# Attention and gate block in one kernel: values ahead of the second softmax with a fixed order of VectorE and GpSimd, front steps in pairs, and products of half of block 2 summed on GpSimd

## Chip, cores, metric

One core of one Trainium2 chip. The metric is the device time of one execution in microseconds (us). Every run that is compared was fast (only one core runs, and no run was over 1.5% above the fastest of its kernel). Engines: PE is TensorE, DVE is VectorE, ACT is ScalarE, POOL is GpSimd, SP issues most transfers.

## The reference, cut

```python
def _A_ref(x, wqkv, wo):                 # S=2048, D=640, 32 heads of 20
    W, dil = 8, 2                        # each position looks at 8 positions, 2 apart, itself and back
    q, k, v = ...(x @ wqkv)
    logits = einsum("bhsd,bhswd->bhsw", q, kg) * Dh**-0.5     # masked where the index is below 0
    attn = softmax(logits, axis=-1)                           # over the 8 offsets
    o = einsum("bhsw,bhswd->bhsd", attn, vg)
    return o.reshape(B, S, D) @ wo
def _B_ref(x, w_gate, w_up, w_down):     # F=1536
    return ((x @ w_gate) * (x @ w_up)) @ w_down
xn = layernorm(x)
return x + _A_ref(xn, wqkv, wo) + _B_ref(xn, w_gate, w_up, w_down)
```

## The kernel before

The sequence is cut into four blocks of 512 positions, 0 to 3. A small scheduler in the kernel's own Python code lists every instruction, orders the engines by modelled durations and sets the semaphores; dependencies come from overlapping memory.

**Logits.** DVE multiplies queries by shifted keys (a product of four offsets at once, 2048 elements). PE sums a product over the 20 columns of each head with a matrix of ones, G, in four 32-column matmuls. There are five chunks of 128 columns; for a half of the offsets in `QUAD`, four of the five are first added in fp32, by GpSimd and by transfers that add to their destination, so that PE has one sum instead of four. Before, that was block 3 alone.

```python
QUAD = {3: (1, 0)}                              # block: halves of the offsets summed on GpSimd
ORDER = ((0, "n"), (1, "n"), (2, "n"), (3, "n"), (3, "w"))
...
for a in range(4):                              # logits(): four 32-column matmuls for each product
    e.matmul(o, G[:], x, start=(i == 0), stop=(i == nt - 1), tile_position=(0, 32 * a))
```

**Softmax.** Blocks 0 and 1 share one logit tile, blocks 2 and 3 the second, LOG1. After a softmax, 16 transfers on SP's queue move the weights into ATX, with the offsets spread over the partitions as the value sums need them.

```python
def move():
    for a in range(4):
        for q in range(4):
            src = L[32 * a:32 * a + 32]...      # L = LOG[x]
            d = ATX[x][32 * q:32 * q + 32]...
            dma(d, src, r=[src], w=[d], ...)
    mark("atx", x)
```

**Shared memory.** Buffers that aren't needed at the same time lie over one another. The gate products of block 2 lie over the two logit tiles. HX0 to HX3 lie over LOG0, HX4 to HX7 over LOG1. The last four gate chunks of block 2 use HX4 to HX7. ACT evacuates gate results into them, and may not do so before the moves out of LOG1 have landed.

```python
LOG = [sb(f"LOG{i}", [128, 2, W, TS]) for i in range(2)]
HX = [sb(f"HX{i}", [128, JB], at=place[0] - 8192 + i * 1024) for i in range(8)]
...
HXM = (0, 1, 2, 3, 8, 9, 10, 11, 4, 5, 6, 7)    # gate chunk of block 2 -> buffer
...
if j == 2 and m == 8:
    yield have("atx", 1)                        # the moves are issued; their landing is a semaphore wait
```

Of the kernel before, what the change touches and what calls it, by code (L numbers as in the profile page):

```python
# [49 lines left out]
class Sched:  # L50
# [5 lines left out]
    def __init__(self, nc):  # L56
# [7 lines left out]
        self.t_lock = 0.0  # L64
        self.t_data = 0.0
# [42 lines left out]
    def deps_of(self, eng, rk, wk):  # L108
# [6 lines left out]
        for k in wk:  # L115
            st = self.state.get(k)
            if st is None:
                continue
            o, rds = st
            if o is not None and not (eng == "pe" and o.eng == "pe"):  # L120
                deps[o.idx] = o
            for q in rds:
                if inorder and q.eng == eng and not q.dma and eng != "dve":
                    continue
                deps[q.idx] = q
        return deps

    def op(self, eng, fn, r=(), w=(), dma=False, name="", occ=None, lat=None, lock=False, nbytes=0, mode=0, group=None, extra=0.0, acc=0.0, land=None):
# [7 lines left out]
        deps = self.deps_of(eng, rk, wk)  # L136
        if occ is None and not dma:
            occ = 0.1
# [45 lines left out]
        if dma:  # L184
# [7 lines left out]
            else:  # L192
                g = self.groups[group]
                g[1].append(X)
                X.event = (g[0], 16)
        self.ops.append(X)
# [152 lines left out]
def build_kernel(nc, A_x, A_wqkv, A_wo, B_x, B_w_gate, B_w_up, B_w_down, out):  # L349
# [43 lines left out]
    sv_free = list(range(NS))  # L393
# [21 lines left out]
    QUAD = {3: (1, 0)}  # L415
# [47 lines left out]
    def dma(o, i, r=(), w=(), name="", eng="sp", group=None, land=None):  # L463
# [10 lines left out]
       r=[IDENT[:]], w=[IDENT[:]], name="ident", occ=0.4)  # L474
    op("pool", lambda e: e.memset(G[:], 0.0), w=[G[:]], name="g0", occ=0.2)
# [58 lines left out]
    def front(t):  # L534
# [11 lines left out]

        def sqrt():
            op("act", lambda e: e.activation(sd, mv[:, 1:2], ACT.Sqrt, bias=EPSC[:, 0:1]), r=[("mv", t), EPSC[:]],  # L548
               w=[("sd", t)], name=f"sd{t}", occ=0.25)
            mark("sd", t)  # L550

        def recip():
            op("dve", lambda e: e.reciprocal(rstd, sd), r=[("sd", t)], w=[("rstd", t)], name=f"rstd{t}", occ=0.16)
            mark("rstd", t)
            if t >= N_DVE_A:
                op("dve", lambda e: e.tensor_scalar(nmr, mv[:, 0:1], rstd, -1.0, op0=ALU.mult, op1=ALU.mult),
                   r=[("mv", t), ("rstd", t)], w=[("nmr", t)], name=f"nmr{t}", occ=0.13)
# [27 lines left out]
        yield Task("act", sqrt, r=[("mv", t)], prio=p - 1)  # L585
        yield Task("dve", recip, r=[("sd", t)], prio=p)
# [192 lines left out]
    def calm():  # L779
        return all(("sm", x) in done or count.get(("logits", x), 0) < 2 for x in range(2))  # L780

    def tokens():
        return [("tok", x) for x in range(2) if ("sm", x) in done]
# [7 lines left out]
    def products():  # L791
        rows = {j: [] for j in range(NJ)}
        holds = {}
        for j, kind in ORDER:
# [4 lines left out]
            else:  # L799
                if len(QUAD.get(j, ())) == 2 and j not in holds:  # L800
# [4 lines left out]
            if len(rows[j]) == 10 - 3 * len(QUAD.get(j, ())):  # L805
                K.spawn(logits(j, rows[j]))

# [17 lines left out]
    def q_bank(j, c, hold):  # L825
# [7 lines left out]
        def copy():  # L833
            evac([(QT[:, j, c, :], PS[:, hold[0], :], JB)], f"qev{j}_{c}")
# [13 lines left out]
    def wide(j, slots, hold):  # L848
        halves = [(r, q0) for r in QUAD[j] for q0 in (0, 2)]
        acc, parts = {}, {1: [], 0: []}  # L850
        for c0 in (0, 2):
            for i, (r, q0) in enumerate(halves):
                f = []
                for c in (c0, c0 + 1):
                    yield lambda: len(hold[c]) > 0 and len(usable(j)) > 0
                    k = slot(j)
# [6 lines left out]
                    def go(o=o, qb=qb, kv=kv, q=q, rk=rk):  # L863
                        X = op("dve", lambda e: e.tensor_tensor(o[:], qb, kv, ALU.mult), r=[q, rk], w=[o[:]],  # L864
# [50 lines left out]
    def logits(j, slots):  # L915
# [7 lines left out]
        def go(*bs):  # L923
            for i, e in enumerate(slots):
                n, s, r = e[:3]
                b, i, nt = bs[1 - r], i - (0 if r else n1), n1 if r else len(slots) - n1
                for a in range(4):
                    o = PS[32 * a:32 * a + 32, b, :].rearrange("p (q s) -> p q s", q=4)
                    x = s[:, :, a * TS:(a + 1) * TS]
                    op("pe", (lambda o, x, i, a: lambda e: e.matmul(o, G[:], x, start=(i == 0), stop=(i == nt - 1),  # L930
                                                                   tile_position=(0, 32 * a)))(o, x, i, a),
# [25 lines left out]
    def softmax(x):  # L957
        def tt(o, a, b, f, name, occ):
            return Task("dve", lambda: op("dve", lambda e: e.tensor_tensor(o, a, b, f), r=[a, b], w=[o], name=name, occ=occ,
                                          lock=True), r=[a, b], w=[o], prio=10, lock=True)  # L960
# [8 lines left out]
        def sub():  # L969
            op("dve", lambda e: e.tensor_tensor(L[:], L[:], bc(M3[:], 8), ALU.subtract), r=[L[:], m3], w=[L[:]], name="lsub",  # L970
               occ=1.2, lock=True)

        def exp():
            op("act", lambda e: e.activation(L[:], L[:], ACT.Exp), r=[L[:]], w=[L[:]], name="exp", occ=1.9)

        def recip():
            op("act", lambda e: e.activation(s3, s3, ACT.Ln), r=[s3], w=[s3], name="rln", occ=0.4)
            op("act", lambda e: e.activation(R, s3, ACT.Exp, scale=-1.0), r=[s3], w=[R], name="rs", occ=0.4)
# [431 lines left out]
```

## Time and profile before

| | before |
|---|---|
| time, median of 4 runs | 268.65 us (268.47 to 268.70) |
| span of the profiled run | 266.8 us |
| start of PE's first transpose, start of its last group | 5.28, 263.72 us |
| second softmax's last multiply starts | 129.75 us |

The prediction below shows the page, PE's waits and the groups. Read the table with them: PE's first transpose to its last group is 258.4 us of the span, and it is nearly gapless in there.

The timeline of ACT shows where the first gate results go into the memory that they read:

```profile
152.11 0.60 ACT L660 ACTIVATE HX<-PS 128x512 bf16<-128x512 f32 x1 [1.56 <-PE PS L1195]
```

This is the ninth of block 2's twelve gate chunks, the first that goes to HX4. In brackets is the idle time before it and what ended it: ACT waited for PE alone. The last move landed at 142.7, 1.9 us after the start of its issue, and had been over for 9.4 us.

### The profile page before, as it was taken

The page shows a single profiled execution, that of the slowest core. Times are in us where ns is not written, and L with a number is a line of the kernel's source. Part 1 is how long each engine was busy: PE and PEld are TensorE (multiplying, and loading weights), DVE is VectorE, ACT ScalarE, POOL GpSimd, SP SyncE. Part 2 cuts the span into 40 slices and gives each one's busy share as a digit, 9 for nine tenths or more (in the row PEclk, how much of TensorE's full clock was granted, in tenths as well). Part 3 has the DMA queues.
Part 4 walks back from the last instruction along what each step waited for, and adds up shares of the span by engine and source line. Part 5 has one row for each costly group of instructions (what it writes and reads, how often), then busy time and mean ns, then how long its engine had stood idle before and what let it go on. Part 6 is the DMA issues. An engine that isn't in the chain of part 4 may idle for free.

```text
span 266.8 us, 4468 instructions
## 1 busy us (share of the span) xinstructions
PE 261.3 (98%) x1771; PEld 152.6 (57%) x1788; DVE 218.3 (82%) x278; ACT 107.6 (40%) x193; POOL 132.4 (50%) x83
## 2 busy tenths in 40 slices
PE   7999999999999999999999999999999999999996
PEld 5996965444444444444444446764577547754775
DVE  4678899999999996379999899988998999981221
ACT  3469998556732122255434442007500460016000
POOL 1000000000007359700399999977999799979000
PEclk9999999999999999999999999999999999999999
DMA  7974789502226997193426733656345633130101
GB/s 213 374 207 81 195 107 371 213 0 98 101 49 161 192 234 178 9 333 81 114 49 142 170 80 87 185 162 168 80 129 152 184 96 89 49 98 2 49 27 49
DMA packets 40933, 35.75 MB, mean 134 GB/s; under 512 B 16080, under 2 KB 39120, under 8 KB 40912
## 3 DMA queue, kind: packets, MB, share of 16 engines
q1 hardware_dynamic: 40096, 33.31, 46.0%
q0 software_dynamic: 576, 2.10, 4.1%
q8 instruction: 14, 0.23, 0.4%
q10 hardware_dynamic: 240, 0.05, 0.1%
q14 instruction: 7, 0.06, 0.1%
HBM read 25.07 MB, written 5.26 MB: 114 GB/s over the span
## 4 chain that ended last, share of the span: by engine, by line
PE 96%; DVE 1%; DMA 1%; issue 1%; ACT 0%
PE PS L1195 39%; PE PS L1277 28%; PE PS L655 22%; PE PS L930 3%; PE PS L687 2%; PE PS L1144 2%; DMA XST<-in_A_x_dram 1%; PE PS L599 0%; DVE STATS L542 0%; ACT XNT L611 0%; DVE XNS L563 0%; DVE XNT L609 0%; DVE FOUT L1290 0%; ACT SD L548 0%; DVE MV L545 0%
## 5 line engine op out<-in xcount | busy, mean ns | idle before, releaser
L1096 POOL TENSOR_TENSOR SV<-PV 128x1024 bf16<-128x1024 f32 x40 | 93.2, 2361 | 20.4 <-DVE LOG L981 19.4
L1091 DVE TENSOR_TENSOR PV<-VX,PS 128x1024 f32<-128x1024 bf16 (+1 forms) x56 | 91.9, 1669 | 2.5 <-POOL SV L1096 2.3
L655 PE MATMUL PS<-XNT,WQKV 128*128 128x512 bf16 (+2 forms) x384 | 60.2, 315 | 0.4 <-issue 0.2
L1195 PE MATMUL PS<-XNT,WG 128*128 128x512 bf16 x238 | 59.4, 379 | 0.2
L1195 PE MATMUL PS<-XNT,WU 128*128 128x512 bf16 x231 | 57.7, 379 | 0.4 <-issue 0.2
L655 PEld LDWEIGHTS PS<-XNT,WQKV 128*128 128x128 bf16 x390 | 37.9, 112 | 21.8 <-ACT LOG L941 0.8
L1195 PEld LDWEIGHTS PS<-XNT,WG 128*128 128x128 bf16 x240 | 23.3, 98 | 28.5 <-issue 0.8
L1195 PEld LDWEIGHTS PS<-XNT,WU 128*128 128x128 bf16 x240 | 23.4, 98 | 28.2 <-ACT LOG L941 0.4
L819 DVE TENSOR_TENSOR PRD<-QT,KT 128x2048 bf16<-128x2048 bf16 x32 | 36.8, 1215 | 0.0
L1290 DVE TENSOR_TENSOR FOUT<-PS,XR 128x320 bf16<-128x320 f32 (+1 forms) x33 | 15.7, 477 | 18.4 <-PE PS L1277 18.3
L1277 PE MATMUL PS<-WD,HT 128*128 128x320 bf16 x192 | 28.5, 299 | 0.0
L660 ACT ACTIVATE HT<-PS 128x512 bf16<-128x512 f32 x24 | 14.3, 596 | 31.6 <-PE PS L1195 31.6
L1277 PE MATMUL PS<-WO,OT 128*128 128x320 bf16 (+1 forms) x165 | 26.6, 295 | 0.0
L890 POOL TENSOR_TENSOR PRF<-PRF,PRF 128x1024 f32<-128x1024 f32 x4 | 9.4, 2348 | 31.2 <-DVE PRF L864 31.2
L660 ACT ACTIVATE UX<-PS 128x512 bf16<-128x512 f32 x14 | 8.4, 597 | 39.5 <-PE PS L1195 39.5
L949 POOL MEMSET LOG<- 32x6 bf16 (+6 forms) x7 | 0.4, 96 | 47.6 <-ACT LOG L941 47.6
L1204 DVE TENSOR_TENSOR HT<-HT,PS 128x512 bf16<-128x512 bf16 x23 | 15.7, 684 | 9.5 <-PE PS L1195 7.4
L1277 PEld LDWEIGHTS PS<-WD,HT 128*128 128x128 bf16 x192 | 18.6, 98 | 8.0 <-issue 0.4
L1277 PEld LDWEIGHTS PS<-WO,OT 128*128 128x128 bf16 x165 | 15.9, 98 | 5.9
L864 DVE TENSOR_TENSOR PRF<-PS,KT 128x1024 f32<-128x1024 f32 x16 | 19.0, 1216 | 0.3 <-DMA PRF<-PRF 0.3
L660 ACT ACTIVATE XNT<-PS 128x512 bf16<-128x512 f32 x12 | 7.2, 598 | 25.5 <-PE PS L1195 25.5
L542 DVE BATCH_NORM_STATS2 STATS<-XST 128x6 f32<-128x320 bf16 x32 | 14.6, 472 | 2.5 <-DMA XST<-in_A_x_dram 2.5
(62 smaller groups left out, 235.7 us busy)
## 6 DMA issues: line engine op xcount, KB each, us to landing
VX<-v_scratch SPq DMA_DIRECT2D x80, 130.0 KB, 2.9
XST<-in_A_x_dram SPq DMA_DIRECT2D x16, 160.0 KB, 5.7
v_scratch<-VST SPq DMA_DIRECT2D x4, 640.0 KB, 4.2
XR<-in_A_x_dram SPq DMA_DIRECT2D x16, 160.0 KB, 2.7
out_dram<-FOUT SPq DMA_DIRECT2D x15, 160.0 KB, 1.8
PRF<-PRF POOLq DMA_DIRECT2D x4, 512.0 KB, 8.7
WG<-in_B_w_gate_dram SPq DMA_DIRECT2D x1, 1920.0 KB, 8.6
WU<-in_B_w_up_dram SPq DMA_DIRECT2D x1, 1920.0 KB, 12.0
```

The costliest lines, as they stand in the source:

```text
L542: op("dve", lambda e: e.bn_stats(o, a), r=[a], w=[("st", t, i)], name=f"bn{t}_{i}", occ=0.49)
L655: op("pe", (lambda o, l, x, c, first: lambda e: e.matmul(o, l, x, start=first, stop=(c == NCH - 1)))(o, l, x, c, first), r=[l, x], w=[o], ...
L660: X = op("act", (lambda o, i: lambda e: e.activation(o, i, ACT.Copy))(o, i), r=[i], w=[o], name=name, occ=0.12 + n * 0.9e-3)
L819: op("dve", lambda e: e.tensor_tensor(s[:], qb, kv, ALU.mult), r=[q, rk], w=[s[:]], name=f"prod{j}_{r}_{c}", occ=1.15, lock=True)
L864: X = op("dve", lambda e: e.tensor_tensor(o[:], qb, kv, ALU.mult), r=[q, rk], w=[o[:]], name=f"prow{j}_{r}_{c}_{q0}", occ=1.17)
L890: yield Task("pool", lambda: op("pool", lambda e: e.tensor_tensor(x, x, y, ALU.add), r=[x, y] + tokens(), w=[x], name=name, occ=2.36, lock ...
L1091: op("dve", lambda e: e.tensor_tensor(p, vw, a, ALU.mult), r=[vv] + rk, w=[p], name=f"pv{u}_{x}_{r0}", occ=0.09 + 1.1 * nr)
L1096: X = op("pool", lambda e: e.tensor_tensor(o, p[:, :, 0, :], p[:, :, 1, :], ALU.add), r=[p[:]] + tokens(), w=[o], name=f"pva{u}_{x}", occ= ...
L1195: op("pe", (lambda l, x, c: lambda e: e.matmul(PS[:, b, :], l, x, start=(c == 0), stop=(c == NCH - 1)))(l, x, c), r=[l, x], w=[PS[:, b, :] ...
L1204: X = op("dve", lambda e: e.tensor_tensor(h, h, PS[:, hold[1], :], ALU.mult), r=[h, PS[:, hold[1], :]], w=[h], name=f"h{m}_{j}", occ=0.65)
L1277: op("pe", (lambda l, x, i: lambda e: e.matmul(dst, l, x, start=(i == 0), stop=(i == n - 1)))(l, x, i), r=[l, x], w=[PS[:, b, :]], name=f" ...
L1290: X = op("dve", lambda e: e.tensor_tensor(o, PS[:, b, 0:wid], xr, ALU.add), r=[PS[:, b, :], xr], w=[o], name=f"fin{t}_{nb}", occ=0.15 + wi ...
```

## The change

The intent: take logit matmuls off PE by adding half of block 2's products on GpSimd, and make room for that. GpSimd stood 19.4 us before the second softmax ended; now its first value sums come before that softmax and between its steps. The order of the DVE and GpSimd instructions that the program marks with `lock` is fixed by semaphores instead of by timing (the port order below, after the program's name `port`). The layer norm's small steps are done for two row tiles at once.

```diff
-    QUAD = {3: (1, 0)}
+    QUAD = {2: (1,), 3: (1, 0)}
-    ORDER = ((0, "n"), (1, "n"), (2, "n"), (3, "n"), (3, "w"))
+    ORDER = ((0, "n"), (1, "n"), (2, "w"), (2, "n"), (3, "n"), (3, "w"))
 ...  (fixed port order: each side waits for what the other issued before)
+        if lock:
+            deps.update({d.idx: d for d in self.port["pool" if eng == "dve" else "dve"]})
 ...  (values may start before the last logits; GpSimd work only where it fits ahead of the next softmax step)
-    def calm():
-        return all(("sm", x) in done or count.get(("logits", x), 0) < 2 for x in range(2))
+    def room(occ, ready=0.0):
+        def f():
+            if count.get(("logits", 0), 0) >= 2 and ("sm", 0) not in done:
+                return False
+            return due[0] == INF or max(K.t["pool"], K.t_lock, ready) + occ <= due[0] + SLIP
+        return f
 ...
     def vx_loads():
-        yield num(NJ, "lg")
+        yield have("products")
 ...  (front in pairs)
+    GROUPS = ((4, 5), (6, 7), (8, 9), (10, 11), (12, 13), (14, 15))
 ...  (the selector SEL is built on GpSimd instead of DVE; further parts cut)
```

More of the change, by code (lines that the diff above doesn't have):

```diff
@@ L64, in __init__ @@
         self.t_lock = 0.0
+        self.port = {"dve": [], "pool": []}
         self.t_data = 0.0
@@ L122, in deps_of @@
             for q in rds:
-                if inorder and q.eng == eng and not q.dma and eng != "dve":
+                if inorder and q.eng == eng and not q.dma and eng != "dve" and not (eng == "act" and k[0] == "ps"):
                     continue
@@ L195, in op @@
                 X.event = (g[0], 16)
+        if lock:
+            self.port[eng] = [X] if eng == "dve" else self.port[eng] + [X]
+            if eng == "dve":
+                self.port["pool"] = []
         self.ops.append(X)
@@ L392, in build_kernel @@
     SV += [sb(f"SV{5 + i}", [128, 4, JB], at=a_ra + i * 4096) for i in range(3)]
-    sv_free = list(range(NS))
+    sv_free = [3, 4, 0, 1, 2]
     a_sc = place[0]
@@ L474, in build_kernel @@
        r=[IDENT[:]], w=[IDENT[:]], name="ident", occ=0.4)
+    op("pool", lambda e: e.memset(SEL[:], 0.0), w=[SEL[:]], name="sel", occ=0.1)
+    for q in range(4):
+        op("pool", (lambda q: lambda e: e.affine_select(SEL[:], SEL[:], pattern=[[-1, 32]], compare_op=ALU.not_equal, fill=1.0,
+                                                        base=-32 * q, channel_multiplier=1))(q),
+           r=[SEL[:]], w=[SEL[:]], name=f"sel{q}", occ=0.2)
     op("pool", lambda e: e.memset(G[:], 0.0), w=[G[:]], name="g0", occ=0.2)
@@ L545, in aggr @@
             op("dve", lambda e: e.bn_aggr(mv, st), r=[("st", t, 0), ("st", t, 1)], w=[("mv", t)], name=f"bnag{t}", occ=0.2)
+        ts = next((g for g in GROUPS if t in g), (t,))
+        t0, t1 = ts[0], ts[-1] + 1
         def sqrt():
-            op("act", lambda e: e.activation(sd, mv[:, 1:2], ACT.Sqrt, bias=EPSC[:, 0:1]), r=[("mv", t), EPSC[:]],
-               w=[("sd", t)], name=f"sd{t}", occ=0.25)
-            mark("sd", t)
+            o, i = SD[:, t0:t1, 0:1], MV[:, t0:t1, 1:2]
+            op("act", lambda e: e.activation(o, i, ACT.Sqrt, bias=EPSC[:, 0:1]), r=[("mv", k) for k in ts] + [EPSC[:]],
+               w=[("sd", k) for k in ts], name=f"sd{t}", occ=0.25)
+            for k in ts:
+                mark("sd", k)
         def recip():
-            op("dve", lambda e: e.reciprocal(rstd, sd), r=[("sd", t)], w=[("rstd", t)], name=f"rstd{t}", occ=0.16)
-            mark("rstd", t)
+            o, i = SD[:, t0:t1, 1:2], SD[:, t0:t1, 0:1]
+            op("dve", lambda e: e.reciprocal(o, i), r=[("sd", k) for k in ts], w=[("rstd", k) for k in ts], name=f"rstd{t}", occ=0.16)
             if t >= N_DVE_A:
-                op("dve", lambda e: e.tensor_scalar(nmr, mv[:, 0:1], rstd, -1.0, op0=ALU.mult, op1=ALU.mult),
-                   r=[("mv", t), ("rstd", t)], w=[("nmr", t)], name=f"nmr{t}", occ=0.13)
+                n, m = SD[:, t0:t1, 2:3], MV[:, t0:t1, 0:1]
+                op("dve", lambda e: e.scalar_tensor_tensor(n, m, -1.0, o, op0=ALU.mult, op1=ALU.mult),
+                   r=[x for k in ts for x in (("mv", k), ("rstd", k))], w=[("nmr", k) for k in ts], name=f"nmr{t}", occ=0.13)
+            for k in ts:
+                mark("rstd", k)
         def apply():
@@ L584, in front @@
         yield Task("dve", aggr, r=[("st", t, 1)], prio=p)
-        yield Task("act", sqrt, r=[("mv", t)], prio=p - 1)
-        yield Task("dve", recip, r=[("sd", t)], prio=p)
+        mark("mv", t)
+        if t == ts[-1]:
+            yield Task("act", sqrt, r=[("mv", t)], prio=p - 1)
+            yield Task("dve", recip, r=[("sd", t)], prio=p)
+        yield have("rstd", t)
         if t >= NXN:
@@ L777, in slot @@
         return n
-    def calm():
-        return all(("sm", x) in done or count.get(("logits", x), 0) < 2 for x in range(2))
+    INF = 1e9
+    due = [INF]
+    def room(occ, ready=0.0):
[4 more added lines that the diff above has]
+        return f
+    calm = room(2.36)
     def tokens():
-        return [("tok", x) for x in range(2) if ("sm", x) in done]
+        return []
     def k_view(j, r, c, q0, nq):
@@ L793, in products @@
         holds = {}
-        for j, kind in ORDER:
+        for at, (j, kind) in enumerate(ORDER):
             if kind == "w":
@@ L799, in products @@
             else:
-                if len(QUAD.get(j, ())) == 2 and j not in holds:
+                if len(QUAD.get(j, ())) == 2 and j not in holds and (j, "w") == ORDER[at + 1]:
                     yield from fetch(j, 0, holds.setdefault(j, {c: [] for c in range(4)}))
@@ L806, in products @@
                 K.spawn(logits(j, rows[j]))
+        mark("products")
     def narrow(j, r, c, slots):
@@ L833, in copy @@
         def copy():
-            evac([(QT[:, j, c, :], PS[:, hold[0], :], JB)], f"qev{j}_{c}")
+            o, i = QT[:, j, c, :], PS[:, hold[0], :]
+            op("act", lambda e: e.activation(o, i, ACT.Copy), r=[i], w=[o, ("qev", j, c)], name=f"qev{j}_{c}", occ=0.58)
             for _ in range(4):
@@ L855, in wide @@
                     yield lambda: len(hold[c]) > 0 and len(usable(j)) > 0
+                    yield num(4, "qk", 0, j, c)
                     k = slot(j)
@@ L863, in go @@
                     def go(o=o, qb=qb, kv=kv, q=q, rk=rk):
-                        X = op("dve", lambda e: e.tensor_tensor(o[:], qb, kv, ALU.mult), r=[q, rk], w=[o[:]],
+                        X = op("dve", lambda e: e.tensor_tensor(o[:], qb, kv, ALU.mult), r=[q, rk, ("qev", j, c)], w=[o[:]],
                                name=f"prow{j}_{r}_{c}_{q0}", occ=1.17)
@@ L929, in go @@
                     x = s[:, :, a * TS:(a + 1) * TS]
-                    op("pe", (lambda o, x, i, a: lambda e: e.matmul(o, G[:], x, start=(i == 0), stop=(i == nt - 1),
-                                                                   tile_position=(0, 32 * a)))(o, x, i, a),
+                    op("pe", (lambda o, x, i, a, nt: lambda e: e.matmul(o, G[:], x, start=(i == 0), stop=(i == nt - 1),
+                                                                   tile_position=(0, 32 * a)))(o, x, i, a, nt),
                        r=[G[:], x], w=[o], name=f"lg{j}_{r}_{i}_{a}", occ=0.054, lat=0.4, mode=1)
@@ L958, in tt, with go @@
         def tt(o, a, b, f, name, occ):
-            return Task("dve", lambda: op("dve", lambda e: e.tensor_tensor(o, a, b, f), r=[a, b], w=[o], name=name, occ=occ,
-                                          lock=True), r=[a, b], w=[o], prio=10, lock=True)
+            def go():
+                X = op("dve", lambda e: e.tensor_tensor(o, a, b, f), r=[a, b], w=[o], name=name, occ=occ, lock=True)
+                due[0] = INF if name == "ssum3" else X.end
+            return Task("dve", go, r=[a, b], w=[o], prio=10, lock=True)
         L = LOG[x]
@@ L971, in sub @@
                occ=1.2, lock=True)
+            due[0] = INF
         def exp():
-            op("act", lambda e: e.activation(L[:], L[:], ACT.Exp), r=[L[:]], w=[L[:]], name="exp", occ=1.9)
+            X = op("act", lambda e: e.activation(L[:], L[:], ACT.Exp), r=[L[:]], w=[L[:]], name="exp", occ=1.9)
+            due[0] = X.end
         def recip():
             op("act", lambda e: e.activation(s3, s3, ACT.Ln), r=[s3], w=[s3], name="rln", occ=0.4)
-            op("act", lambda e: e.activation(R, s3, ACT.Exp, scale=-1.0), r=[s3], w=[R], name="rs", occ=0.4)
+            X = op("act", lambda e: e.activation(R, s3, ACT.Exp, scale=-1.0), r=[s3], w=[R], name="rs", occ=0.4)
+            due[0] = X.end
         def attn():
-            op("dve", lambda e: e.tensor_tensor(L[:], L[:], bc(RS[:], 8), ALU.mult), r=[L[:], R], w=[L[:], ("tok", x)], name="attn",
+            op("dve", lambda e: e.tensor_tensor(L[:], L[:], bc(RS[:], 8), ALU.mult), r=[L[:], R], w=[L[:]], name="attn",
                occ=1.2, lock=True)
+            due[0] = INF
         def move():
@@ L992, in softmax @@
         yield num(2, "logits", x)
+        if x:
+            due[0] = max([0.0] + [d.end for d in K.deps_of("dve", K.keys(L[:]), ()).values()])
         if x:
@@ L1040, in weighted @@
         yield have("atx", 0)
+        yield have("products")
         def take(a, b):
@@ L1045, in weighted, with at_copy @@
         yield Task("act", take, banks=2, prio=0, contig=True)
+        for r in range(2):
+            yield Task("act", lambda: at_copy(0, r), r=[ATX[0][:, 0, r, :]], w=[PS[:, at_bank[r], :]], prio=1)
         for u in range(NU):
             yield from unit(u)
+    def at_copy(j, r):
+        o, i = PS[:, at_bank[r], :], ATX[j // 2][:, j % 2, r, :]
+        op("act", lambda e: e.activation(o, i, ACT.Copy), r=[i], w=[o], name=f"atp{j}_{r}", occ=0.55)
     def unit(u):
@@ L1056, in unit @@
             sv_free.extend(range(NS, len(SV)))
-        yield lambda: len(sv_free) > 0
+        yield lambda: len(sv_free) > 0 and (sv_free[0] in (3, 4) or count.get(("lg",), 0) >= NJ)
         sv_of[u] = sv_free.pop(0)
@@ L1072, in unit @@
         v = VX[:, u % NVX]
-        def at_copy(r):
-            o, i = PS[:, at_bank[r], :], ATX[j // 2][:, j % 2, r, :]
-            op("act", lambda e: e.activation(o, i, ACT.Copy), r=[i], w=[o], name=f"atp{j}_{r}", occ=0.55)
         def mul(x, r0, nr):
@@ L1108, in adder @@
             yield Task("pool", lambda: add(x), r=[slots[x][:]], w=[sv[:, 2 * x:2 * x + 2, :]], prio=10, lock=True)
-        if c in (0, NCH - 1):
+        if c == NCH - 1 or (c == 0 and j):
             for r in range(2):
                 if c == 0:
-                    yield Task("act", lambda: at_copy(r), r=[ATX[j // 2][:, j % 2, r, :]],
+                    yield Task("act", lambda: at_copy(j, r), r=[ATX[j // 2][:, j % 2, r, :]],
                                w=[PS[:, at_bank[r], :]], prio=1)
@@ L1163, in on_pool @@
     def on_pool(j, m):
-        return ("sm", 1) in done and m < 11 and ucount[0] - count.get(("hp",), 0) < HP_MAX
+        return count.get(("lg",), 0) >= NJ and m < 11 and ucount[0] - count.get(("hp",), 0) < HP_MAX
     def gu(j):
@@ L1220, in pmul @@
                     def pmul():
-                        op("pool", lambda e: e.tensor_tensor(h, h, us, ALU.mult), r=[h, us], w=[h], name=f"hp{m}_{j}",
+                        op("pool", lambda e: e.tensor_tensor(h, h, us, ALU.mult), r=[h, us] + tokens(), w=[h], name=f"hp{m}_{j}",
                            occ=1.15, lock=True)
@@ L1227, in after @@
                     yield num(k0, "hp")
-                    yield calm
+                    yield room(1.15)
                     yield Task("pool", pmul, r=[h, us], w=[h], prio=HP_PRIO, lock=True)
@@ L1238, in xr_loads @@
     def xr_loads():
-        yield have("xnt", NT - 1)
+        yield num(NJ, "lg")
         yield have("vx", NVX)
@@ L1311, in dn_piece @@
         K.spawn(tail())
+    SLIP = 0.3
     N_PE_T = 4
     BN_AFTER = (4,)
+    GROUPS = ((4, 5), (6, 7), (8, 9), (10, 11), (12, 13), (14, 15))
     N_DVE_A = 6
@@ L1341, in misc @@
         yield have("xnt", NT - 1)
-        def sel():
-            for q in range(4):
-                a, b = SEL[32 * q:32 * q + 32, :], IDENT[32 * q:32 * q + 32, 32 * q:32 * q + 32]
-                op("dve", (lambda a, b: lambda e: e.tensor_copy(a, b))(a, b), r=[b], w=[a], name=f"sel{q}", occ=0.1)
         def preload(e):
@@ L1351, in misc @@
         free.append(NPR - 1)
-        yield Task("dve", sel, prio=19)
         yield Task("act", lambda: op("act", preload, name="exp_preload", occ=1.3), prio=6)
```

## The prediction

> **What bounds the kernel now.** I read the page's busy shares and slices first, then the waits of TensorE (PE), the chain that ended last, the groups by shape and at last the timeline of each engine between 100 and 165 us.
>
> The page, busy shares and slices:
>
> ```profile
> span 266.8 us, 4468 instructions
> ...
> PE 261.3 (98%) x1771; PEld 152.6 (57%) x1788; DVE 218.3 (82%) x278; ACT 107.6 (40%) x193; POOL 132.4 (50%) x83
> ...
> PE   7999999999999999999999999999999999999996
> ...
> DVE  4678899999999996379999899988998999981221
> ...
> POOL 1000000000007359700399999977999799979000
> ...
> PEclk9999999999999999999999999999999999999999
> ```
>
> PE is busy in every slice and its clock is fully granted; VectorE (DVE) and GpSimd (POOL) have holes in the middle: after POOL's first burst come two empty slices and one at 3 tenths, about 113 to 133 us (a slice is 6.67 us).
>
> Whether those holes matter is told by the waits of PE, all of them (what is waited for, us in total, times, longest):
>
> ```profile
> PE PS L639 <- DVE ZERO L469: 1.3, 1, 1.3
> PE PS L687 <- DVE XNT L609: 0.3, 1, 0.3
> PE PS L655 <- issue: 0.2, 1, 0.2
> PE PS L1195 <- issue: 0.2, 1, 0.2
> ```
>
> Only 0.4 us of them come after the start, and those two are not waits for another engine. The chain that ended last is 96% PE. As a check I counted PE's instructions in the program order and priced them with start-to-start steps of the timeline (five 512-column matmuls 1.08 us, so 0.216 each; twelve plus five of 320 columns 2.31 us, so 0.136 each; forty logit matmuls 2.27 us): 257.2 us of work lie in the 259.0 us between the first transpose (5.28) and the last sum (264.27). So the kernel before has at most 1.8 us of PE gaps in all, most of them in the first 14 us. Nothing that the other engines do better can be worth more.
>
> [...] forty 32-row logit matmuls of 512 columns take 2.27 us, 0.057 each, about a quarter of 0.216. [...] 2048 bf16 elements and 1024 with fp32 and PSUM cost the same. [...]
>
> Groups by shape (busy us, mean ns of one, then idle before):
>
> ```profile
> L819 DVE TENSOR_TENSOR PRD<-QT,KT 128x2048 bf16<-128x2048 bf16 x32 | 36.8, 1215 | 0.0
> ...
> L864 DVE TENSOR_TENSOR PRF<-PS,KT 128x1024 f32<-128x1024 f32 x16 | 19.0, 1216 | 0.3 <-DMA PRF<-PRF 0.3
> ...
> L930 PE MATMUL PS<-PRD,G 128*32 128x512 bf16 x136 | 8.1, 380 | 0.0
> ```
>
> **The change, part by part.**
> *Half of block 2 summed over chunks.* Logit matmuls go from 136 to 124: four products become one, three times four matmuls fall away. 12 x 0.0568 = 0.68 us off PE, the only PE work that changes: the 512-column projections stay 200 (the Q chunks of block 2 only move), the sums by SEL stay 80 in the same five groups[...]. DVE pays: 8 new half products at 1.216 less 4 whole ones at 1.215, +4.9 us. POOL pays four more sums of 2.35 (+9.4) and two more accumulating transfers, issued in 0.9 us each and landing 8.1 to 8.9 us after issue.
> *Front.* Square root, reciprocal and shift for two row tiles at once: reciprocals 16 to 10, shifts 10 to 5, so 6 x 0.163 + 5 x 0.214 = 2.05 us of DVE busy time, and about five stops of 0.17 us at the reciprocals. SEL moves to POOL (-0.70 DVE). The first product should start at about 32 instead of 34.3 us. PE isn't waiting there. Row tiles 0 to 3, which do set PE's start, keep their order; tiles 4 on arrive in pairs, 4 and 5 landing near 23 us by my count against about 24.7 where PE wants them.
> *Port order and values ahead of softmax 2.* This is for POOL's hole. Timelines of POOL, DVE and PE (start, length, instruction, idle before):
>
> ```profile
> 107.00 4.64 POOL L908 TENSOR_TENSOR PRD<-PRF,PRF 128x1024 bf16<-128x1024 f32 x2
> 131.05 16.26 POOL L1096 TENSOR_TENSOR SV<-PV 128x1024 bf16<-128x1024 f32 x7 [19.41 <-DVE LOG L981]
> ```
>
> ```profile
> 110.52 0.69 DVE L1204 TENSOR_TENSOR HT<-HT,PS 128x512 bf16<-128x512 bf16 x1 [1.47 <-PE PS L1195]
> 112.68 0.69 DVE L1204 TENSOR_TENSOR HT<-HT,PS 128x512 bf16<-128x512 bf16 x1 [1.47 <-PE PS L1195]
> ```
>
> ```profile
> 114.66 1.05 PE L930 MATMUL PS<-PRD,G 128*32 128x512 bf16 x16
> ...
> 141.64 0.61 PE L1144 MATMUL PS<-SV,SEL 128*32 128x512 bf16 x8
> ```
>
> POOL stands 19.4 us until softmax 2's last multiply, and DVE stands 1.47 us of each 2.16 from 104 to 115. In the changed order POOL adds the first units before and between the steps of softmax 2. That fills the hole, but PE at 114.66 and 141.64 wasn't waiting for either, so the 19.4 us are worth nothing by themselves: they pay for the 10 us that POOL gets in addition (with one more gate product), and give slack.
>
> Sum: -0.68 on PE, 0 from the front, 0 from the hole: 268.65 - 0.68 = 267.97, **268.0 us**. Busy times should be PE 260.6, DVE about 219.7 (218.3 + 4.9 - 2.05 - 0.7 - 0.7 for a gate product that goes to POOL), POOL about 146 (132.4 + 9.4 + 1.8 + 1.2 + some 1 for SEL).
>
> **Does PE now wait?** I followed the changed program order with the durations above. PE's times are its work before that point plus 6 us (6.5 late). Products for block 2 are ready near 86 and its POOL sums near 83; PE wants them at 88.6. The last product of block 3 is done near 113.6, POOL's last sum near 122.3 (it waits for accumulating transfers); PE wants it at 124.9 to 125.4 (before: 111.6 against 114.7, the same 3 us). The first two value units: 137 against 140. The next three: about 160.7 against 161.7, one microsecond, where in the kernel before it was about 2 (157.7 against 159.6). Later groups have more room than before, since POOL started some 10 us earlier.
>
> **Rivals.**
> *A new wait on PE.* The fixed order makes a DVE product stand behind a POOL sum, and that sum behind a transfer of over 8 us. For it: one product of block 2 comes right behind such a sum (about 83.05 against 82.8 wanted), and the slack at the third deadline is 1 us, less than the error of my count. Against it: the gate matmuls fill PE in between, and the kernel before keeps such deadlines with 1 to 3 us of slack and no PE wait. It would cost 0.5 to 2 us: 268.5 to 270.
> *DVE or POOL becomes the bound.* That needs their work to slip from unit to unit up to the end. DVE rises by about 1.4 us to some 220 of 266, POOL to some 146, both gain filled holes, and DVE's last slices are at 1 and 2 tenths. Near nothing: if so, 271 or more.
> *The hole was the bound and the gain is large.* A change named for values ahead of softmax invites it: up to 10 us off. PE's 98% and 0.4 us of waits speak against it; the floor is 268.65 less 1.8 of gaps less 0.68, or 266.2.
>
> **Range and chances.** Seven in ten for the bare 0.68 with a few tenths either way; two in ten for a new PE wait up to 1.5 us; the rest for something unforeseen at the start or more. So 267.4 to 269.3. Faster by over 2% would be under 263.3, below the floor: 0.01. Slower by over 2% is above 274.0, which needs 6 us of PE waits: 0.02.
>
> **What would show it.** Right: PE's waits still under 1 us after the start, PE busy down by about 0.7 with logit matmuls x124, the chain still some 96% PE, POOL's 19.4 us wait gone or cut into waits of a few us, and the span down by about 0.7. Wrong: a PE wait on PRD or SV near 88, 125, 140 or 161 us (the rival of the new wait); PE gaps at 24 us (pairs in the front); or a span that falls by more than 1.5 us, which would mean that PE had lost time in a form its records don't show.

The forecast: its sum is -0.68 us on PE, 0 from the front and 0 from the hole, 268.65 - 0.68 = 267.97. What the trace of before shows: 0.057 us for a logit matmul (forty in 2.27 us) against 0.216 for one on all 128 columns, and 1215 ns for 2048 bf16 elements on DVE against 1216 for 1024 in fp32 from PSUM. The 1 us for SEL on GpSimd was an estimate; in the changed kernel it took 0.97 us there (four instructions of 0.212 and one of 0.120) against 0.66 on DVE before (four of 0.165).

## More of the kernel before

One more view became important later, the timeline of SP's queue (start, length, then what was issued):

```profile
128.89 1.74 SPq L467 DMA_DIRECT2D VX<-v_scratch  x4
...
131.15 10.27 SPq L467 DMA_DIRECT2D ATX<-LOG  x16
```

The sixteen moves out of LOG1 keep the queue for 10.3 us, 0.64 each, and the last is issued from 140.8 to 141.4.

## The result and the profile after

| | before | after |
|---|---|---|
| time, median of 4 runs each | 268.65 us (268.47 to 268.70) | 268.99 us (268.73 to 269.16) |
| ratio | | 1.0013, 95% interval 0.9996 to 1.0030: the same |
| span of the profiled run | 266.8 us | 267.6 us |
| PE, start of first transpose to start of last group | 258.44 us | 259.09 us |
| logit matmuls | 136 | 124 |

A ratio is the mean time of one kernel's fast runs over that of the other's fast runs of the same rounds, so it isn't quite the ratio of the medians. All outputs are right. In a later comparison the changed kernel stood at 1.0019 (1.0006 to 1.0031), so it is a little slower, not equal (experiment e10).

The page after, its first parts and the chain by engine:

```profile
span 267.6 us, 4440 instructions
...
PE 261.2 (98%) x1760; PEld 152.5 (57%) x1776; DVE 218.8 (82%) x264; ACT 106.1 (40%) x188; POOL 145.7 (54%) x95
...
PE   7999999999999999999999998999999999999996
...
POOL 3000000012453252899465996999999899979000
...
PE 76%; ACT 7%; DVE 7%; SPq 4%; issue 2%; DMA 2%; POOL 1%; DVEq 0%; ACTq 0%
```

GpSimd's empty slices in the middle are filled. PE's row has a slice at 8 where it had 9 before, some 160 to 167 us. The chain fell from 96% PE to 76%. That does not mean that PE limits a fifth less. The chain is followed backwards, and one late wait of PE leads it away through ACT, DVE and SP's queue. Some matmul records are missing (1760 of 1776), so PE's busy time can't be compared to tenths.

PE's waits after (what is waited for, us in total, times, longest):

```profile
PE PS L662 <- DVE ZERO L476: 1.3, 1, 1.3
PE PS L1325 <- DVE HX L1252: 0.8, 1, 0.8
PE PS L678 <- issue: 0.4, 2, 0.2
PE PS L710 <- DVE XNT L632: 0.3, 1, 0.3
```

The second line is new. L1325 is the down projection; its bank is released by DVE's gate product L1252. The groups by shape show that the intended part did happen:

```profile
L900 DVE TENSOR_TENSOR PRF<-PS,KT 128x1024 f32<-128x1024 f32 x24 | 28.3, 1215 | 2.0 <-ACT QT L869 2.0
...
L966 PE MATMUL PS<-PRD,G 128*32 128x512 bf16 x124 | 7.4, 380 | 0.0
```

There are 24 half products instead of 16, and 124 logit matmuls instead of 136. In GpSimd's list of waits the 19.4 us ahead of the first value sum are gone. Value sums now wait 3.3, 2.9 and less, and they start at 122.94 instead of 131.05.

So where did PE's gain go? The time is followed back from PE's stop at 163 us, in the timelines of PE, DVE, ACT and SP's queue:

```profile
161.68 0.83 PE L1192 MATMUL PS<-SV,SEL 128*32 128x512 bf16 x12
163.31 1.80 PE L1325 MATMUL PS<-WD,HT 128*128 128x320 bf16 x12 [0.80 <-DVE HX L1252]
```

```profile
158.22 1.22 DVE L1139 TENSOR_TENSOR PV<-VX,PS 128x1024 f32<-128x1024 bf16 x1 [3.15 <-ACT PS L1099]
...
162.57 0.68 DVE L1252 TENSOR_TENSOR HX<-HX,PS 128x512 bf16<-128x512 bf16 x1
```

```profile
149.62 0.60 ACT L683 ACTIVATE HX<-PS 128x512 bf16<-128x512 f32 x1 [1.56 <-PE PS L1243]
156.60 1.08 ACT L683 ACTIVATE HX<-PS 128x512 bf16<-128x512 f32 x2 [6.38 <-DMA ATX<-LOG]
157.57 0.61 ACT L1099 ACTIVATE PS<-ATX 128x512 f32<-128x512 bf16 x1
```

```profile
133.06 10.92 SPq L474 DMA_DIRECT2D VX<-v_scratch  x8
144.01 11.23 SPq L474 DMA_DIRECT2D ATX<-LOG  x16
```

Read from the last fence upwards. The moves out of LOG1 are issued from 144.0 to 155.2, some 13 us later than before. ACT comes to its first evacuation into HX4 at 150.2 and stands 6.4 us, because HX4 is memory that the moves still read. (For the first 1.4 us of them PE's result isn't there either: in e1 below, where nothing else is waited for, the same evacuation runs at 151.64.) Behind it in ACT's stream stands the copy of the weights (L1099) that DVE's next value product needs; DVE stands 3.15 us. The gate products behind that one are late, PE's bank is late, and PE stops for 0.8 us at 163. A smaller stop is at 157 (0.3 us on ACT's evacuation, by name in the repeat e10).

Why the moves are later: the logits of block 3 stand 10.5 us later in PE's order (125.12 against 114.66), and the second softmax is now spread between value work. Its last multiply starts at 142.13 instead of 129.75. The line of the logits after, and of that multiply before and after:

```profile
125.12 1.05 PE L966 MATMUL PS<-PRD,G 128*32 128x512 bf16 x16
```

```profile
129.75 1.22 DVE L981 TENSOR_TENSOR LOG<-LOG,RS 128x2048 bf16<-128x2048 bf16 x1
...
142.13 1.22 DVE L1023 TENSOR_TENSOR LOG<-LOG,RS 128x2048 bf16<-128x2048 bf16 x1
```

The sums of block 2, with the half products that DVE has to make for them, set this shift: without them (e2 below) the logits stand at 110.98 and the multiply at 131.00. This is the theory that the experiments test: the gain of 12 matmuls was there, and it was lost to a wait for memory that HX4 to HX7 share with LOG1.

The rival at this point: the extra DVE and GpSimd work, or the fixed port order, slows things in the middle by itself, and the wait on the moves is only where it happens to show.

### The profile page after: what moved, and what is told of

The parts are those of the page before. It is cut to its first block, busy times and chain, and to the rows that moved or that the text cites. A ratio compares the mean times of both kernels' runs of the same rounds, so it can differ in the third digit from the quotient of the medians.

```text
span 267.6 us, 4440 instructions
## 1 busy us (share of the span) xinstructions
PE 261.2 (98%) x1760; PEld 152.5 (57%) x1776; DVE 218.8 (82%) x264; ACT 106.1 (40%) x188; POOL 145.7 (54%) x95
## 3 DMA queue, kind: packets, MB, share of 16 engines
q0 software_dynamic: 864, 3.15, 6.2%
## 4 chain that ended last, share of the span: by engine, by line
PE 76%; ACT 7%; DVE 7%; SPq 4%; issue 2%; DMA 2%; POOL 1%; DVEq 0%; ACTq 0%
PE PS L1243 30%; PE PS L1325 28%; PE PS L678 12%; SPq L474 4%; ACT XNS L589 3%; PE PS L710 2%; PE PS L966 2%; DVE PRF L900 2%; DVE PV L1139 1%; PE PS L1192 1%; DMA XST<-in_A_x_dram 1%; POOL PRF L926 1%; DVE SM L996 1%; ACT VST L683 1%; DMA ATX<-LOG 1%
## 5 line engine op out<-in xcount | busy, mean ns | idle before, releaser
L1144 POOL TENSOR_TENSOR SV<-PV 128x1024 bf16<-128x1024 f32 x40 | 93.5, 2362 | 11.4 <-DVE PV L1139 3.8
L1243 PE MATMUL PS<-XNT,WU 128*128 128x512 bf16 x236 | 59.1, 379 | 0.3
L1243 PE MATMUL PS<-XNT,WG 128*128 128x512 bf16 x233 | 58.1, 379 | 0.5 <-issue 0.2
L853 DVE TENSOR_TENSOR PRD<-QT,KT 128x2048 bf16<-128x2048 bf16 x28 | 32.2, 1221 | 1.8 <-POOL PRF L926 1.3
L900 DVE TENSOR_TENSOR PRF<-PS,KT 128x1024 f32<-128x1024 f32 x24 | 28.3, 1215 | 2.0 <-ACT QT L869 2.0
L1325 PE MATMUL PS<-WD,HT 128*128 128x320 bf16 x192 | 28.6, 299 | 0.8 <-DVE HX L1252 0.8
L926 POOL TENSOR_TENSOR PRF<-PRF,PRF 128x1024 f32<-128x1024 f32 x6 | 14.1, 2354 | 23.2 <-DVE PRF L900 19.8
L1325 PE MATMUL PS<-WO,OT 128*128 128x320 bf16 (+1 forms) x165 | 26.6, 295 | 0.0
L1325 PEld LDWEIGHTS PS<-WD,HT 128*128 128x128 bf16 x192 | 18.6, 98 | 8.9 <-DVE HX L1252 1.3
L1252 DVE TENSOR_TENSOR HT<-HT,PS 128x512 bf16<-128x512 bf16 x22 | 15.0, 683 | 6.4 <-PE PS L1243 6.2
L1325 PEld LDWEIGHTS PS<-WO,OT 128*128 128x128 bf16 x165 | 15.9, 98 | 5.9
L944 POOL TENSOR_TENSOR PRD<-PRF,PRF 128x1024 bf16<-128x1024 f32 x6 | 14.0, 2357 | 4.4 <-DVE PRD L853 4.2
```

The costliest lines, as they stand in the source:

```text
L853: op("dve", lambda e: e.tensor_tensor(s[:], qb, kv, ALU.mult), r=[q, rk], w=[s[:]], name=f"prod{j}_{r}_{c}", occ=1.15, lock=True)
L900: X = op("dve", lambda e: e.tensor_tensor(o[:], qb, kv, ALU.mult), r=[q, rk, ("qev", j, c)], w=[o[:]], name=f"prow{j}_{r}_{c}_{q0}", occ=1.17)
L926: yield Task("pool", lambda: op("pool", lambda e: e.tensor_tensor(x, x, y, ALU.add), r=[x, y] + tokens(), w=[x], name=name, occ=2.36, lock ...
L944: yield Task("pool", lambda: op("pool", lambda e: e.tensor_tensor(o, a, y, ALU.add), r=[a, y] + tokens(), w=[o], name=f"qend{j}_{r}_{q0}", ...
L1144: X = op("pool", lambda e: e.tensor_tensor(o, p[:, :, 0, :], p[:, :, 1, :], ALU.add), r=[p[:]] + tokens(), w=[o], name=f"pva{u}_{x}", occ= ...
L1243: op("pe", (lambda l, x, c: lambda e: e.matmul(PS[:, b, :], l, x, start=(c == 0), stop=(c == NCH - 1)))(l, x, c), r=[l, x], w=[PS[:, b, :] ...
```

## The experiments

Three calls, eleven runs, each call on one chip with runs of the kernel before between. Medians of before: 268.75 us (e1 to e4), 268.48 (e5 to e8), 268.47 (e9 to e11).

### e1: the four buffers on other memory

```diff
-    HX = [sb(f"HX{i}", [128, JB], at=place[0] - 8192 + i * 1024) for i in range(8)]
+    HX = [sb(f"HX{i}", [128, JB], at=place[0] - 8192 + i * 1024 if i < 4
+             else a_ot + 3 * NCH * JB * 2 + (i - 4) * 1024) for i in range(8)]
```

The new place is the last block of the attention output OT, which is not in use then. PE's order of instructions is the same as in the changed kernel.

> The changed kernel, but the gate products of block 2 whose buffers lie over the second logit tile (chunks 8 to 11) get other memory: the part of the value output that block 3 fills last. PE's order is unchanged. Theory 1 (PE lost time because ScalarE stood 6.4 us in front of that memory, until the moves of the attention weights out of it had landed): ScalarE's wait goes, PE's waits on the gate products at 157 and 163 us go, 1.1 us: 267.7 to 268.0 us. Rival 2 (softmax 2 and the values are simply later and VectorE is too full at 155 to 163 us): PE still waits there for VectorE, 268.7 to 269.1.

Measured: 267.93 us (267.88 to 268.34), ratio to before 0.9975 (0.9961 to 0.9988). The moves are issued as late as in the changed kernel (143.87 to 154.8), but ACT no longer asks:

```profile
151.64 0.60 ACT L683 ACTIVATE HX<-PS 128x512 bf16<-128x512 f32 x1 [1.56 <-PE PS L1243]
153.80 0.60 ACT L683 ACTIVATE HX<-PS 128x512 bf16<-128x512 f32 x1 [1.56 <-PE PS L1243]
154.29 0.59 ACT L1099 ACTIVATE PS<-ATX 128x512 f32<-128x512 bf16 x1
```

PE has no wait on HX left. From its first transpose to its last group are 257.77 us: 0.67 less than before, and 1.32 less than in the changed kernel. By these two profiles the memory shared with the moves cost 1.3 us, 1.1 of it in the two stops of PE; by the medians of e10 and e11 below it cost 1.0. Either is more than the loss against the kernel before (0.3 to 0.5 us), since it also took the gain of the twelve matmuls.

### e3 and e4: the moves made later on purpose

Eight small loads go on SP's queue just ahead of the second softmax's moves, in the changed kernel (e3) and in e1 (e4).

```diff
         def move():
+            for i in range(8 if x else 0):
+                d = TCH[32 * (i % 4):32 * (i % 4) + 32, i // 4, :]
+                stores.append(op("sp", lambda e, d=d: e.dma_start(d, xhbm[0:32, 0:32]), w=[d], dma=True, occ=0.0))
```

> The changed kernel with 8 tiny loads put in front of the second softmax's moves on the sync engine's queue, nothing else moved. They delay the landing by some 4 to 5 us. Theory 1: ScalarE's stop grows from 6.4 to some 11 us, and since PE's margin is used up, nearly all of it reaches PE: 272 to 274 us. Rival 2: the moves matter to nobody before block 2's values, 269.0 to 269.3.

Measured for e3: 274.14 us (273.56 to 274.77), ratio 1.0203 (1.0186 to 1.0219). The moves start at 148.92, 4.9 us later than in the changed kernel; ACT stands 9.7 us and PE 3.4:

```profile
156.56 1.24 PE L1247 MATMUL PS<-XNT,WU 128*128 128x512 bf16 x5
161.22 1.25 PE L1247 MATMUL PS<-XNT,WG 128*128 128x512 bf16 x5 [3.42 <-ACT HX L684]
162.31 2.26 PE L1247 MATMUL PS<-XNT,WU 128*128 128x512 bf16 x5
164.36 1.96 PE L1247 MATMUL PS<-XNT,WG 128*128 128x512 bf16 x5
```

A delay of 4.9 us cost 5.2 us (274.14 against 268.99; the profiled spans differ by 4.6), although PE's stops grew by only 2.3 us (from 0.3 and 0.8 to 3.4). Most of the rest is in the last two lines: five matmuls take 2.26 and 1.96 us instead of 1.24, 1.7 us more together. The table by windows gives PE a granted clock of 0.57 from 162 to 166 us, and 1.00 from 166 to 170. The 0.8 us stop of the changed kernel left the clock at 1.00 (160 to 166 us). The fall came late: the first five matmuls after the stop still took 1.25 us, and the slow ones start at 162.31, 1.1 us after PE ran again.

> The same 8 tiny loads in the kernel of the first run (other memory for the four gate products). Theory 1: no one waits for the moves any more, so the delay costs nothing: as the first run within 0.3 us, unless the loads of the values behind them on the same queue come too late. Rival 2: also no change, but from 269.0.

Measured for e4: 267.90 us (267.87 to 268.04), ratio 0.9971 (0.9957 to 0.9984). The moves are as late as in e3 (148.82), and the time is that of e1. So lateness of the moves costs nothing except through the shared buffers. This pair tells the theory from the rival.

### e2 and e5: without the sums of block 2

```diff
-    QUAD = {2: (1,), 3: (1, 0)}
-    ORDER = ((0, "n"), (1, "n"), (2, "w"), (2, "n"), (3, "n"), (3, "w"))
+    QUAD = {3: (1, 0)}
+    ORDER = ((0, "n"), (1, "n"), (2, "n"), (3, "n"), (3, "w"))
```

e2 is this edit in the changed kernel, e5 in e1.

> The changed kernel without its summed half of block 2 (front pairs, port order and values ahead stay; the reused memory stays). The logit matmuls are x136 again (+0.68 us of PE work). Theory 1: the third block's logits and softmax 2 come some 14 us earlier by PE's order, the moves land before ScalarE wants the memory, no wait of PE on gate products: 268.5 to 268.9, as the kernel before. Rival 3 (port order or values ahead themselves cost PE time): 269.3 or more, with PE waits left.

> The kernel of e1 (the four gate products of block 2 moved off the second logit tile) without the added sums of block 2: 136 logit matmuls again instead of 124, everything else of the change and the moved buffers kept. If what e1 won over the kernel before is the 12 matmuls of 56.8 ns and nothing else, this run gives it back: some 0.7 us more than e1, so 268.5 to 268.8, the same as the kernel before within 0.1%. Rival: the moved buffers or the fixed port order are a gain of their own; then this run lies with e1 at 267.9 to 268.1. No wait of TensorE on HX over 0.3 us in either case.

Measured: e2 268.68 us (268.51 to 269.07), ratio 1.0002 (0.9989 to 1.0014); e5 268.46 us (268.44 to 268.56), ratio 0.9999 (0.9987 to 1.0011). Both take as long as the kernel before. Two things follow. Pairs, port order and early values are together worth nothing without the sums. And the shared buffers alone are harmless: in e2 they lie over LOG1 too, but the last multiply of the softmax starts at 131.00, the moves at 132.24, and ACT has no wait on them. It takes the later logits *and* the overlap. The whole gain of e1 comes with the twelve matmuls: from first transpose to last group e5 has 258.40 us and e1 257.77, a difference of 0.63. Each of these is one profile, and one profile is not sure to tenths: e2's has 259.16 between the same marks, 0.43 of it a stop at 8 us for a row tile of the layer norm.

### e6: the pairs of the front alone

The kernel before with `GROUPS` and the three paired steps, nothing else.

> The kernel before with one part of the change alone: the front's small VectorE steps (inverse deviation and the scaled mean) done for two row tiles at once. VectorE should lose about 2 us of busy time, from 217.5 to some 215.5 us, and TensorE should neither gain nor wait: 268.5 to 268.8. Rival: the front's VectorE steps lie on the path of TensorE's start, so that the time falls by 0.3 us or more, or a pair's later second half makes the transposes wait and the time rises by 0.3 us or more.

Measured: 268.88 us (268.48 to 268.97), ratio 1.0011 (0.9999 to 1.0023). DVE's busy time fell to 214.8 us, 3.5 less than before's 218.3, more than expected, because two more gate products went to GpSimd too (DVE has 32 instead of 34, GpSimd 85 instructions instead of 83). The median is 0.1 us above the range that I gave, and PE's list of waits has none for another engine over 0.4 us, apart from the 1.3 at the start that before has too. One of 0.39 us at 8.2 us, for a normed row tile (`XNS`), is new. Nine of the eleven profiles with the pairs have such a stop (0.2 to 0.6 us), and neither of the two without them (before, e7); why was not tested. The interval includes 1, so whether pairs cost some 0.3 us by themselves stays open; they gain nothing. The changed kernel without the pairs was not run: the kernel's scheduler finds no order for it as it stands. With `DN_KEEP = 5`, as in e7 to e9, the kernel does build, so this test stood open.

### e7: the sums of block 2 alone

The kernel before with `QUAD` and `ORDER` of the change and what they need in `wide` and `logits`, without pairs, port order and early values. The kernel's scheduler finds no order with `DN_KEEP = 3` (a bank kept free), so this has 5; that alone changes no instruction of the kernel before or of e1, as a comparison of their built programs showed.

> The kernel before with the sums of block 2 alone: no pairs in the front, no fixed port order, no values ahead of softmax 2, and one bank more kept free ahead of the last sums so that the kernel's scheduler finds an order at all. 124 logit matmuls. If the extra products and sums need the rest of the change to find time on VectorE and GpSimd, TensorE waits on them and the time is 269 to 272. If not, it is 267.9 to 268.2 and the rest of the change was not needed for the gain. A wait of ACT on the moves into the second logit tile would again stand ahead of its HX evacuation, since the four buffers lie there too.

Measured: 279.66 us (278.44 to 281.66), ratio 1.0435 (1.0400 to 1.0470). The direction is the first one that I named, but the size is far beyond my 272. ACT stands 6.3 us on the moves, as expected, and PE 1.9 us on HX for it. Then PE waits 5.5 us for value sums near the end (`SV`, two stops, which end at 254 and 256), with the clock at 0.50 from 254 to 258. I had left out the lower clock, which e3 had shown after its stop (0.57 from 162 to 166 us).

### e9: everything of e1 except the early values

Sums of block 2, pairs and moved buffers kept; the fixed port order, the values ahead of the softmax and the selector on GpSimd left out, `DN_KEEP = 5`.

> e1 without one part: sums of block 2, pairs in the front and moved gate products are kept; the fixed port order, the values ahead of the second softmax and the selector built on GpSimd are left out (and one bank more is kept free ahead of the last sums, which alone changes no instruction in the kernel before or in e1). Theory, from e7: GpSimd's stop of 18 to 19 us ahead of its first value sum comes back, that sum starts only after the second softmax, at 140 us or later instead of some 123, GpSimd is behind until the end and TensorE waits for value sums (SV) of block 3 near 250 us by 3 to 6 us[...]. So 272 to 277. Rival: what made e7 slow was the VectorE work that the pairs save and the gate products' memory; then this run is at 267.9 to 268.5 with no wait on SV.

A clause is cut from it that put a general statement about the clock after such a wait, and with it a term of the sum: 1.5 to 2.5 us for slower matmuls. The 272 to 277 is e1's 267.9 plus the wait of 3 to 6 us plus that term. The two runs before it show its size: in e3 ten matmuls took 1.7 us more (granted clock 0.57 from 162 to 166 us), and in e7, after stops of 3.79 and 1.69 us, seventeen of 320 columns took 3.83 us from start to start instead of 2.31 (0.50 from 254 to 258).

Measured: 275.41 us (275.31 to 275.65), ratio 1.0259 (1.0245 to 1.0273), as the theory had it. The timelines of GpSimd and of PE:

```profile
141.22 16.24 POOL L1109 TENSOR_TENSOR SV<-PV 128x1024 bf16<-128x1024 f32 x7 [18.54 <-DVE LOG L994]
```

```profile
249.28 0.39 PE L1157 MATMUL PS<-SV,SEL 128*32 128x512 bf16 x2 [1.54 <-POOL SV L1109]
251.58 0.61 PE L1157 MATMUL PS<-SV,SEL 128*32 128x512 bf16 x2 [1.91 <-POOL SV L1109]
```

GpSimd's stop of 18.5 us is back, its first value sum comes at 141.2 instead of 122.8 in e1, and 108 us later PE pays for it: 3.4 us of stops, and then matmuls at a lower clock (0.52 from 250 to 254 us, 0.63 from 254 to 258; the first twelve of 320 columns took 3.41 us instead of 1.79). So the parts that fill the hole, which were worth nothing with 136 logit matmuls (e2, e5), are worth 7 us once the second softmax ends later. Which of the port order and the early values is needed for it this run can't tell, because they were left out together.

### e8: one step more

e1 with `QUAD = {2: (1, 0), 3: (1, 0)}` and `DN_KEEP = 5`: 112 logit matmuls.

> The kernel of e1 with one step more of the same kind: both halves of the offsets of block 2 summed on GpSimd, 112 logit matmuls instead of 124, with one bank more kept free ahead of the last sums. If TensorE still waits for nothing, another 12 times 56.8 ns goes: 0.7 us below e1, 267.2 to 267.4. Rival: VectorE and GpSimd have no room left for 12 more products and three more sums before the second softmax, the values come late and TensorE waits: 268.5 or more, with waits on SV, HX or PRD of 1 us or more in the list of TensorE's waits.

Measured: 274.03 us (273.75 to 275.19), ratio 1.0214 (1.0196 to 1.0232). My first number missed, and the rival came true. The softmax's last multiply starts at 151.06, 9 us later than in e1; PE waits 3.4 us for value sums at 249 and 251, and again the clock falls (0.59 from 250 to 254). One step beyond e1 is more than VectorE and GpSimd can carry with this order.

### e10 and e11: the changed kernel and e1 again, on one chip

> The changed kernel itself, again, beside e11 on one chip: 268.7 to 269.1, and about 0.1% above the kernel before of the same rounds. If it were below the kernel before by 0.1% or more, the loss seen in the first comparison would be noise of the chip.

> e1 itself, again, beside e10 on one chip: 267.8 to 268.0, 0.8 to 1.2 us below e10 and 0.6 to 0.9 us below the kernel before of the same rounds.

Measured: the changed kernel 269.01 us (268.64 to 269.37), ratio 1.0019 (1.0006 to 1.0031); e1 268.00 us (267.69 to 268.13), ratio 0.9979 (0.9965 to 0.9993). They are 1.0 us apart on one chip. ACT stands 6.6 us on the moves in e10 and not at all in e11. e10 is 0.5 us above before instead of the 0.3 that I expected. e1 is the version that beats both kernels, by 0.2% (before) and 0.4% (changed).

## Why the prediction was right, and where it was wrong

The range held (268.99 in 267.4 to 269.3) and the class (the same, within 2%) was right. The point, 268.0, was 1.0 us low, and its sign was wrong: a small loss came instead of a small gain. That the range held is in part luck: it had room for a wait of PE up to 1.5 us, and one of that size came from a place where the prediction didn't look. Of its own signs for being right, the 124 logit matmuls and the cut wait of GpSimd came; the chain at 96% PE (it was 76%) and the span down by 0.7 us (it rose by 0.8) did not, and PE's waits after the start came to more than 1 us.

- **What bounds the kernel: right.** What the change moved in the time shows as PE's own work and stops, and no run came below the floor of 266.2 (the fastest, in e11, took 267.69).
- **-0.68 us for twelve matmuls: right.** It is the difference between e1 and before in PE's own times (0.67), and between e1 and e5 (0.63). The timed medians give 0.82 (e1) and 0.47 us (e11). With single profiles and medians that spread so far, the agreement to 0.05 us is closer than the method can show.
- **0 from the front, 0 from the hole: right for the kernel before**, shown by e2 and e5. The half sentence that the hole "pays for" GpSimd's added work turned out to be the larger point: without it the sums cost 7 us (e9).
- **DVE and GpSimd busy: right.** 218.8 against some 219.7, and 145.7 against 146.
- **Deadlines for products and value sums: right.** PE came to the logits of blocks 2 and 3 at 88.86 and 125.12 us (predicted 88.6 and 124.9 to 125.4), to the first value sums at 140.2 (140) and to the next at 161.68 (161.7), and waited at none of them. GpSimd's last product sum ended at 123.0 (122.3). The ready times of the value sums were less exact: 139.4 for the first two units (137 predicted, so 0.8 us of slack and not 3) and 159.6 for the next (160.7). The accumulating transfers landed in 4.5 to 4.7 us, not in the 8.1 to 8.9 that the prediction took over from before.
- **The step that failed: "Does PE now wait?".** It listed what PE reads, products and value sums, and the wait came from what PE's results are written to. The logits of block 3 had moved by 10.5 us, and the sum of that step didn't ask who waits for the softmax other than the value sums. LOG1 has to be empty before ACT may write HX4 to HX7. Before, the moves had landed by 142.7 and were needed at 152.1, 9.4 us of slack. In the changed kernel they landed 13.8 us later, at 156.5, for an evacuation that could run at 151.6 (e1's time for it), a miss of 5 us. One more deadline in the list, with numbers that the profile of before and the changed order held, would have shown it. The prediction saw a wait on "PRD or SV near 88, 125, 140 or 161 us"; it was on HX at 157 and 163.
- **The rival of the new PE wait** was what happened, in size (0.5 to 2 us; 1.0 to 1.3 came) and time (268.5 to 270). Its mechanism was another: not the port order behind a slow transfer, but memory reuse through ACT's stream and SP's queue. It got two chances in ten, too few for a check that left out one kind of dependency.

Not shown: why a DVE stop of 3.15 us became 0.8 us at PE and not more. The gate products behind it took up the rest; I read that from the timelines and didn't vary it.

## What to carry to other kernels

When a change delays one result, list every reader and also every later writer of the memory that the result lies in, and give each a deadline; here a write that had to wait for a read cost more than the change gained (1.0 to 1.3 us against 0.7), and moving four small buffers brought the gain back. An idle hole that costs nothing now is a reserve, and a change that shifts work later may need it. A stop of TensorE is not always paid by its length alone: after the stop of 3.42 us in e3 the clock fell (0.57 from 162 to 166 us), and ten matmuls took 1.7 us more than before.

## What else the traces show

- Stops shorter than e3's 3.42 us were also followed by a lower clock: in e9 stops of 1.54 and 1.91 us, with two matmuls of 0.39 us between them, by a granted clock of 0.52 from 250 to 254 us, and in e8 the same two lengths by 0.59. A single stop of 1.9 us in e7 was not (1.00 from 155 to 165 us and from 165 to 180). What decides it stays open.
- Each of the sixteen 32 KB moves held SP's queue for 0.60 us (median) and landed 1.9 us (median) after the start of its issue, and the sixteen together took 10.3 to 11.4 us to issue. So most of the time to the last landing was issue: in the kernel before 10.3 us, and the last landed 1.9 us after the start of its own.
- The 512 KB transfers that accumulate landed in a median of 8.7 us in the kernel before and 4.5 us in the changed one. Runs without the sums of block 2 have 9.2 us (e2) and 8.7 (e6), runs with them 4.5 (e1, e3, e9); no run varied what lay beside them, so the cause stays open.
